# Attention: the queries' scale moves from the turning copies to the maximum pass, and the last queries move into the keys' tile

## The chip, the cores and the metric

The kernel runs on one core of one Trainium2 chip. The metric is the device time of one execution in microseconds (us); the median of several runs is compared. Engines are named as in the profile: PE (TensorE; PEld is its weight load), DVE (VectorE), ACT (ScalarE), POOL (GpSimd), SP (SyncE, which issues most transfers).

## What is computed

```python
batch, n_heads, seq, head_dim = (8, 8, 576, 64)
scale = 1.0 / np.sqrt(q.shape[-1])
scores = scale * np.matmul(q, k.transpose(0, 1, 3, 2))
thresh = np.max(scores, axis=-1, keepdims=True) - tau
scores = np.where(scores >= thresh, scores, -1000000000.0)
attn = exp(scores - max), divided by (its row sum + 1e-9)
x = (attn @ v), heads side by side: 4608 tokens x 512
h = np.maximum(x @ w_in, 0.0)          # 512 -> 2048
return (h * h @ w_out)                 # 2048 -> 512
```

All of it is computed in fp32. The two weight matrices arrive in a wide type and are converted in the kernel while the attention runs.

## The kernel before

The program has two stages, one after the other. The first is the attention, the second the two dense layers, done by a scheme that trades matrix products for sums. The change touches the attention alone.

**Units and periods.** A pair is one batch with two neighbouring heads (j = 0, 1), 32 in all. A unit is 128 queries of a pair (4 units a pair) or the last 64 queries of two pairs together; there are 144 units. A period handles two units, A and B, and also the end of earlier ones, so that there are 72 periods. What each engine gets in a period, and in which order, is written out by hand: `PLAIN` (L592) and `CONVERTING` (L597). CONVERTING is taken by the 33 periods in which weights are converted (periods 2 to 34, since two halves of a conversion lie in neighbouring periods), PLAIN by the 37 after them; periods 0 and 1 have lists of their own (`BEGIN_WITH`, L602). Every engine works through its own queue in this order; semaphores join them.

**The steps of a period.** 
- `SA` and `SB` (`scores`, L423): PE multiplies queries by keys into PSUM (`sc`, six banks). A's 576 scores per row lie in bank 0 (j = 0) and bank 5 (j = 1), with the last 64 in bank 1 or 4; B's lie in banks 2 and 3.
- `topA0` and its three fellows (`top`, L450, instruction L452): DVE reads 576 scores of a row from PSUM, writes them to SBUF (tile `s`), and accumulates the row's minimum. The scores are negated, because the scale is negative.
- `leastA` (L459, POOL) makes the threshold; `powA0` (L462, ACT) the exponentials; `maskA0` (L467, DVE) compares with the threshold, which is a value per row, multiplies, and accumulates the row's sum.
- `U`, `V`, `W` (L380, L515, PE) turn the weights 64 by 64 into PSUM, and `eU`, `eV`, `eW` (L523, ACT) copy them out.
- `PV` (L532, PE) multiplies by the values into banks 0 and 5, so it has to come behind topA0 and topA1. `x` (L659 on DVE in PLAIN, L657 on ACT in CONVERTING) copies the result out.
- `T` (`turn`, L391, instruction L398) turns the queries or the keys of a coming pair on PE, into banks 1 and 4. `eT` copies them out (L403 and L411). For queries (`which` 0) that is two ACT activations of 128x256 with the scale (L403); for keys (`which` 1) two plain ACT copies of 256 and 320 columns (L411) and one ACT activation of 64 columns (L403), the pair's last 64 queries. In the very first turn of keys DVE makes the second copy.

**Where things lie.** Turned queries are `qT` (512 columns), keys `kT` (576 columns), the last queries `qR` (64 columns). `qscale` is a column of 128 values, -1/8 for a tau that isn't negative; `read_tau` (L114) makes it at the start. The line that the maximum pass has now is

```python
made = nc.vector.tensor_scalar(
    out=s[:, j, :], in0=sc[:, ds(at, S)], scalar1=1.0, scalar2=None,
    op0=ALU.mult, op1=ALU.min, accum_out=nmx[:, j : j + 1],
)
```

Of the kernel before, what the change touches and what calls it, by code (L numbers as in the profile page):

```python
# [10 lines left out]
FP32 = mybir.dt.float32  # L11
# [3 lines left out]
AF = mybir.ActivationFunctionType  # L15
# [33 lines left out]
def kernel(  # L49
# [25 lines left out]
    nc = tc.nc  # L75
    B, H, S, D = q.shape
    P = 128
# [3 lines left out]
    FULL = S // P  # L81
    REST = S - FULL * P
    BLK = [P] * FULL + [REST]
    NB = len(BLK)
    BANK = 512
    MAIN = FULL * P
# [16 lines left out]
    sb, cv = Region(arena, 0, X_AT[0]), Region(arena, X_AT[0], ARENA)  # L103
# [7 lines left out]
    qscale = const.tile([P, 1], FP32, name="qscale")  # L111
# [160 lines left out]
    loaded, loaded_v, turned, weights = {}, {}, {}, {}  # L272
    CH = NB + FULL
    HALF = P // 2
# [57 lines left out]
    def places(i):  # L332
        if i not in turned:
            turned[i] = (
                sb.tile([P, MAIN], FP32, tag="qT", bufs=Q_RING, name="qT"),
                sb.tile([P, S], FP32, tag="kT", bufs=K_RING, name="kT"),
                sb.tile([P, REST], FP32, tag="qR", bufs=K_RING, name="qR"),
            )
        return turned[i]

# [2 lines left out]
    def ask_ahead(i, which):  # L343

        while asked[which] < min(len(pairs) - 1, i + (2 if i else 1)):
            asked[which] += 1
            (load_k if which else load_q)(asked[which])
# [4 lines left out]
    Q_RING, K_RING, W_RING = 3, 4, 2  # L352
    MEET = (("scores", "turned", (Q_RING, K_RING)), ("values", "weights", (W_RING,)), ("x", "weights", (W_RING,)))

    def touch(what, made, at, size, key=0):

        if at is None:
            return
        on = range(at // BANK, (at + size - 1) // BANK + 1)
        met = {made.ins.engine}  # L360
        for kind, other, others, its in reversed(touched):
            e = other.ins.engine
            if e == made.ins.engine:
                continue
            if on[-1] < others[0] or others[-1] < on[0]:
                if any({what, kind} == {x, y} and any((key - its) % n == 0 for n in rings) for x, y, rings in MEET):
                    continue
                tc.declare_no_dep(made.ins, other.ins, reason="other banks")
            elif e not in met:
                met.add(e)  # L370
                tc.add_manual_dep(made.ins, other.ins.name, behind, reason="same bank")
        touched.append((what, made, on, key))
        while len(touched) > 300:
            touched.popleft()
# [16 lines left out]
    def turn(i, which, spots, other=None):  # L391

        nat, to = loaded.pop((i, which)), places(i)
        of = [nat[:, t, :] for t in range(FULL)] + ([loaded.pop((i, 2))] if which else [])
        for t, x in enumerate(of):
            for r, (spot, at) in enumerate(spots):
                rows = ds(r * HALF, HALF)
                made = nc.tensor.transpose(spot[:, ts(t, HALF)], x[rows, :], ident[rows, rows])  # L398
                touch("turns", made, at, BANK)
        half = FULL * HALF  # L400

        def scaled(to, spot):
            touch("turned", nc.scalar.activation(out=to, in_=spot[0], func=AF.Identity, scale=qscale[:, :]), spot[1], BANK, i)  # L403

        def then():
            part = lambda r, x, n: (spots[r][0][:, ds(x, n)], spots[r][1])
            if which:
                for r, n in ((0, half), (1, half + REST)):
                    spot = part(r, 0, n)
                    copy_by = other if r and other else nc.scalar.copy  # L410
                    touch("turned", copy_by(to[1][:, ds(r * half, n)], spot[0]), spot[1], BANK, i)  # L411
                scaled(to[2], part(0, half, REST))
                ask_ahead(i, 1)
            else:
                for r in range(2):
                    scaled(to[0][:, ds(r * half, half)], part(r, 0, half))
                ask_ahead(i, 0)

        return then

# [2 lines left out]
    def scores(n, rest):  # L423

        of, t = units[n]
        at_k, count = (MAIN, REST) if rest else (0, MAIN)
        for j in range(2):
            first = n % 2 != j
            to = (3 * j + 1) * BANK + first * (BANK - REST) if rest else (3 * j + 2 * first) * BANK
            for c in range(2):  # L430
                rows, at = ds(j * D, D), ds(c * HALF, HALF)
                qT, kT, qR = turned[of[c]]
                lhs = qT[rows, ds((c * FULL + t) * HALF, HALF)] if t < FULL else qR[rows, :]
                made = nc.tensor.matmul(  # L434
                    sc[at, ds(to, count)], lhs, kT[rows, ds(at_k, count)], start=True, stop=True
                )
                touch("scores", made, to, count, of[c])

    def softmax(n):

        if n % 2 == 0:
            smalls[n // 2] = sb.tile([P, 4, 4], FP32, tag="small", bufs=4, name="small")
        small = smalls[n // 2]
        nmx, thr, sm = (small[:, i, ds(n % 2 * 2, 2)] for i in range(3))
        w = sb.tile([P, CH, 2, D], FP32, tag="w", bufs=4, name="w")
        s = sb.tile([P, 2, S], FP32, tag="s", bufs=2, name="s")
        weights[n] = w
        of = lambda j: s[:, j, :].rearrange("p (c d) -> p c d", d=D)

        def top(j):  # L450
            at = 3 * j * BANK + (n % 2 != j) * (2 * BANK - REST)
            made = nc.vector.tensor_scalar(  # L452
                out=s[:, j, :], in0=sc[:, ds(at, S)], scalar1=1.0, scalar2=None,
                op0=ALU.mult, op1=ALU.min, accum_out=nmx[:, j : j + 1],
            )
            touch("tops", made, at, S)

        def least():
            nc.gpsimd.tensor_scalar(out=thr, in0=nmx, scalar1=tau_p[:, :], scalar2=None, op0=ALU.add)  # L459

        def power(j):
            nc.scalar.activation(  # L462
                out=w[:, :, j, :], in_=of(j), func=AF.Exp, bias=nmx[:, j : j + 1], scale=-1.0
            )

        def mask(j):
            nc.vector.scalar_tensor_tensor(  # L467
                out=w[:, :, j, :], in0=of(j), scalar=thr[:, j : j + 1], in1=w[:, :, j, :],
                op0=ALU.is_le, op1=ALU.mult, accum_out=sm[:, j : j + 1],
            )  # L470

        def over():
            sm = small[:, 2, :]
            nc.gpsimd.tensor_scalar(out=sm, in0=sm, scalar1=1e-9, scalar2=None, op0=ALU.add)

        def inverse():
            nc.vector.reciprocal(out=small[:, 3, :], in_=small[:, 2, :])

        soft[n] = dict(top=top, least=least, power=power, mask=mask, over=over, inverse=inverse)

    def do(n, what, *args):
# [6 lines left out]
    for g in range(2, 2 * len(pairs)):  # L488
        two, x = divmod(g - 4, 4)
# [129 lines left out]
    def period(p):  # L619
# [19 lines left out]
        def turn_some():  # L639
            free = None  # L640
            if turns and p < 2:
                pq = pt_pool.tile([P, 2, BANK], FP32, tag="pt", name="pq")
                free = [(pq[:, r, :], None) for r in range(2)]
            late["turn"] = [turn(g // 2, g % 2, free or spots()) for g in turns]
# [30 lines left out]
        def scored_a():  # L675
            if has(A):
                scores(A, False)
                scores(A, True)
                scores(B_, True)
                softmax(A)  # L680
# [438 lines left out]
    with tc.manual_schedule():  # L1119
        with ExitStack() as stack:  # L1120
            sc = stack.enter_context(tc.tile_pool(name="sc", bufs=1, space=PSUM)).tile([P, 6 * BANK], FP32, name="sc")
# [114 lines left out]
        for n, (steps, h) in enumerate(PASSES):  # L1236
# [106 lines left out]
```

## Time and profile before

| | |
|---|---|
| runs (us) | 1298.04, 1300.32, 1300.54; median 1300.32 |
| profiled execution, first to last instruction (us) | 1298.2; no other time of it is listed |
| granted TensorE clock, mean | 0.997 |
| busy over the span | PE 98%, PEld 86%, DVE 78%, ACT 65%, POOL 71% |
| attention | to about 496 us; DVE busy 229.03 of 232 us in 20 to 252, 235.39 of 244 us in 252 to 496 |
| two dense layers | from about 496 us; PE busy 792.81 of 802.2 us |

A busy share tells how much of a stretch an engine had an instruction in it; it doesn't tell who waits for whom. For that, the order of one period's instructions in time is read.

### The profile page before, as it was taken

Reading aid. Unit: us, or ns where it says so; the run is one execution under the profiler, and the core shown is the slowest. Engines: PE = TensorE matmul, PEld = TensorE weight load, DVE = VectorE, ACT = ScalarE, POOL = GpSimd, SP = SyncE. Lnnn points to the kernel's source line nnn. Section 1 sums busy time; section 2 is a strip of 40 time slices with the busy share of each in tenths; the row PEclk is TensorE's granted clock in tenths of the full one; section 3 lists DMA queues with packets and bytes.
Section 4 is the critical chain, followed back from the end, with each engine's and each line's share of the span. In section 5 each row is a group of like instructions: output and inputs, shape, how many; then the busy total and the mean of one; then the engine's idle time right before and its main releaser. Section 6 shows DMA issues by size and latency. Waiting matters only on the chain.

```text
span 1298.2 us, 45819 instructions
## 1 busy us (share of the span) xinstructions
PE 1276.4 (98%) x18287; PEld 1117.7 (86%) x18287; DVE 1007.0 (78%) x2423; ACT 845.5 (65%) x1498; POOL 926.8 (71%) x1031
## 2 busy tenths in 40 slices
PE   8999999999999999999999999999999999999998
PEld 5777777677777778988888888999999999999998
DVE  6999999999999996886887878867646654665463
ACT  6999999888998984666765856675523432343240
POOL 2787878755555321888897989858787767777775
PEclk8999999999999999999999999999999999999999
DMA  5665566544333312667768768589554224522411
GB/s 143 163 160 154 153 192 180 149 103 110 85 79 80 92 34 64 191 183 218 212 186 226 218 175 235 162 304 391 195 159 164 83 86 159 163 80 88 160 34 34
DMA packets 291413, 196.20 MB, mean 151 GB/s; under 512 B 100096, under 2 KB 252160, under 8 KB 291200
## 3 DMA queue, kind: packets, MB, share of 16 engines
q1 hardware_dynamic: 289888, 192.87, 51.5%
q8 instruction: 144, 2.36, 0.8%
q14 instruction: 69, 0.57, 0.2%
q10 hardware_dynamic: 1312, 0.41, 0.1%
HBM read 120.85 MB, written 72.35 MB: 149 GB/s over the span
## 4 chain that ended last, share of the span: by engine, by line
PE 86%; ACT 5%; DVE 4%; DMA 3%; issue 2%; POOL 0%; SPq 0%; ACTq 0%; DVEq 0%; POOLq 0%
PE po L1077 28%; PE ph L935 16%; PE sc L532 11%; PE sc L434 10%; PE ph L942 10%; PE pt L380 6%; DVE arena L452 2%; PE sc L515 2%; PE sc L398 2%; ACT arena L462 1%; ACT arena L523 1%; DMA g<-arena 1%; PE sc L380 1%; DVE arena L125 1%; DMA wall<-w 1%
## 5 line engine op out<-in xcount | busy, mean ns | idle before, releaser
L125 POOL TENSOR_TENSOR arena<-arena 128x512 f32<-128x512 f32 (+1 forms) x314 | 378.1, 1222 | 147.0 <-DVE arena L125 119.3
L1077 PE MATMUL po<-wall,arena 128*128 128x128 f32 x3528 | 395.0, 275 | 1.9 <-ACT arena L752 1.4
L1077 PEld LDWEIGHTS po<-wall,arena 128*128 128x128 f32 x3528 | 394.4, 192 | 2.5 <-ACT arena L752 1.8
L125 DVE TENSOR_TENSOR arena<-ph,arena 128x512 f32<-128x512 f32 x378 | 255.1, 689 | 79.9 <-PE ph L935 31.5
L122 POOL TENSOR_TENSOR arena<-arena 128x128 f32<-128x128 f32 (+1 forms) x322 | 265.4, 825 | 23.0 <-DMA arena<-w 6.6
L935 PE MATMUL ph<-arena,wall 128*128 128x256 f32 x1176 | 256.6, 380 | 1.8 <-DVE arena L125 1.4
L935 PEld LDWEIGHTS ph<-arena,wall 128*128 128x128 f32 x1176 | 222.2, 190 | 35.9 <-DVE arena L125 5.4
L125 DVE TENSOR_TENSOR arena<-po,arena 128x128 f32<-128x128 f32 x378 | 108.2, 290 | 167.7 <-PE po L1077 163.4
L467 DVE SCALAR_TENSOR_TENSOR arena<-arena 128x576 f32<-128x576 f32 x288 | 235.7, 855 | 0.9 <-ACT arena L462 0.9
L791 ACT COPY c<-arena 128x512 f32<-128x512 f32 (+1 forms) x295 | 169.0, 578 | 71.8 <-DVE arena L122 35.8
L452 DVE TENSOR_SCALAR_CACHE_REDUCE arena<-sc 128x576 f32<-128x576 f32 x288 | 205.1, 748 | 10.9 <-ACT arena L523 4.3
L462 ACT ACTIVATE arena<-arena 128x576 f32<-128x576 f32 x288 | 208.7, 773 | 7.4 <-DVE arena L452 4.2
L532 PEld LDWEIGHTS sc<-arena 64*64 64x64 f32 x5760 | 159.2, 133 | 36.5 <-DVE arena L452 19.8
L532 PE MATMUL sc<-arena 64*64 64x128 f32 (+1 forms) x5760 | 180.5, 262 | 2.9 <-DVE arena L452 1.3
L434 PE MATMUL sc<-arena 64*64 64x64 f32 (+1 forms) x2304 | 176.2, 415 | 3.8 <-ACT arena L403 2.4
L523 ACT COPY arena<-pt 128x1024 f32<-128x1024 f32 x144 | 146.4, 1016 | 27.9 <-PE pt L380 26.5
L122 DVE TENSOR_TENSOR arena<-arena,c 128x512 f32<-128x512 f32 x235 | 154.4, 666 | 11.0 <-ACT c L791 7.6
L752 ACT COPY arena<-po 128x128 f32<-128x128 f32 x63 | 16.6, 264 | 186.4 <-PE po L1077 183.7
L942 PE MATMUL ph<-arena,wall 128*128 128x128 f32 x1176 | 132.0, 275 | 0.7 <-DVE arena L659 0.7
L942 PEld LDWEIGHTS ph<-arena,wall 128*128 128x128 f32 x1176 | 131.6, 192 | 1.1 <-issue 0.8
L380 PEld LDWEIGHTS pt<-ident,arena 64*128 64x128 f32 x2304 | 83.5, 139 | 40.0 <-ACT arena L523 30.1
L434 PEld LDWEIGHTS sc<-arena 64*64 64x64 f32 x2304 | 74.0, 134 | 42.2 <-issue 14.1
(54 smaller groups left out, 1079.7 us busy)
## 6 DMA issues: line engine op xcount, KB each, us to landing
arena<-g SPq DMA_DIRECT2D x144, 256.0 KB, 4.4
g<-arena SPq DMA_DIRECT2D x192, 128.0 KB, 2.9
w<-arena SPq DMA_DIRECT2D x60, 256.0 KB, 2.8
wall<-w SPq DMA_DIRECT2D x49, 256.0 KB, 5.2
g<-arena SPq DMA_DIRECT2D x48, 256.0 KB, 3.8
arena<-w SPq DMA_DIRECT2D x44, 256.0 KB, 3.3
arena<-in_v_dram SPq DMA_DIRECT2D x32, 288.0 KB, 3.8
out_dram<-arena SPq DMA_DIRECT2D x70, 128.0 KB, 2.2
```

What stands on the lines that cost most here:

```text
L122: e.tensor_tensor(out=out, in0=x, in1=y, op=ALU.subtract)
L125: e.tensor_tensor(out=out, in0=x, in1=y, op=ALU.add)
L380: made = nc.tensor.transpose(pt[:, r, ts(slot, HALF)], of[rows, :], ident[rows, rows])
L434: made = nc.tensor.matmul(sc[at, ds(to, count)], lhs, kT[rows, ds(at_k, count)], start=True, stop=True)
L452: made = nc.vector.tensor_scalar(out=s[:, j, :], in0=sc[:, ds(at, S)], scalar1=1.0, scalar2=None, op0=ALU.mult, op1=ALU.min, accum_out=nmx ...
L462: nc.scalar.activation(out=w[:, :, j, :], in_=of(j), func=AF.Exp, bias=nmx[:, j : j + 1], scale=-1.0)
L467: nc.vector.scalar_tensor_tensor(out=w[:, :, j, :], in0=of(j), scalar=thr[:, j : j + 1], in1=w[:, :, j, :], op0=ALU.is_le, op1=ALU.mult, a ...
L532: made = nc.tensor.matmul(sc[ds(u * D, D), ds(5 * j * BANK + row, count)], loaded_v[i][rows, (c - (u != j)) % CH, :], wT[m][rows, ds(weigh ...
L791: nc.scalar.copy(c, y)
L935: nc.tensor.matmul(to[:, 2 * j : 2 * j + 2, :], W_IN[m, k][:, ts(2 * h + j, P)], part_x(steps, k, m), start=(not more and j == 0), stop=Tr ...
L942: nc.tensor.matmul(to[:, j, :], W_IN[m, k][:, ts(j, P)], x, start=(not more and j == 0), stop=True, skip_group_check=True,)
L1077: nc.tensor.matmul(to, g[:, j, :], w[:, j, :], start=(not more and j == 0), stop=(j == 3), skip_group_check=True)
```

## The change

The maximum pass multiplies by `qscale`, a column in SBUF, where it multiplied by the constant 1.0. The turned queries are no longer scaled: `eT` is two plain ACT copies for queries (256 columns each) and two for keys (320 columns each). The keys' tile gets 640 columns in two halves of 320: the first half ends with the pair's last 64 queries, the second with the last 64 keys. So the keys that a main score product reads are two pieces of 256 columns with a gap of 64. `qR` is gone; the SBUF taken is the same. PE, POOL and SP have the same instructions in the same order; DVE has the same instructions, the 288 of L452 with another operand; ACT has 32 fewer.

```diff
-                sb.tile([P, MAIN], FP32, tag="qT", bufs=Q_RING, name="qT"),
-                sb.tile([P, S], FP32, tag="kT", bufs=K_RING, name="kT"),
-                sb.tile([P, REST], FP32, tag="qR", bufs=K_RING, name="qR"),
+                sb.tile([P, 2, MAIN // 2], FP32, tag="qT", bufs=Q_RING, name="qT"),
+                sb.tile([P, 2, MAIN // 2 + HALF], FP32, tag="kT", bufs=K_RING, name="kT"),
...
-            if which:
-                for r, n in ((0, half), (1, half + REST)):
-                    spot = part(r, 0, n)
-                    copy_by = other if r and other else nc.scalar.copy
-                    touch("turned", copy_by(to[1][:, ds(r * half, n)], spot[0]), spot[1], BANK, i)
-                scaled(to[2], part(0, half, REST))
-                ask_ahead(i, 1)
-            else:
-                for r in range(2):
-                    scaled(to[0][:, ds(r * half, half)], part(r, 0, half))
-                ask_ahead(i, 0)
+            for r, (spot, at) in enumerate(spots):
+                copy_by = other if r and other else nc.scalar.copy
+                touch("turned", copy_by(to[which][:, r, :], spot[:, 0 : len(of) * HALF]), at, BANK, i)
+            ask_ahead(i, which)
...
-                lhs = qT[rows, ds((c * FULL + t) * HALF, HALF)] if t < FULL else qR[rows, :]
+                lhs = qT[rows, c, ts(t, HALF)] if t < FULL else kT[rows, 0, MAIN // 2 :]
+                into, rhs = sc[at, ds(to, count)], kT[rows, 1, MAIN // 2 :]
+                if not rest:
+                    into, rhs = into.rearrange("p (r n) -> p r n", r=2), kT[rows, :, 0 : MAIN // 2]
...
-                out=s[:, j, :], in0=sc[:, ds(at, S)], scalar1=1.0, scalar2=None,
+                out=s[:, j, :], in0=sc[:, ds(at, S)], scalar1=qscale[:, :], scalar2=None,
```

More of the change, by code (lines that the diff above doesn't have):

```diff
@@ L399, in turn @@
                 touch("turns", made, at, BANK)
-        half = FULL * HALF
-        def scaled(to, spot):
-            touch("turned", nc.scalar.activation(out=to, in_=spot[0], func=AF.Identity, scale=qscale[:, :]), spot[1], BANK, i)
         def then():
-            part = lambda r, x, n: (spots[r][0][:, ds(x, n)], spots[r][1])
-            if which:
-                for r, n in ((0, half), (1, half + REST)):
-                    spot = part(r, 0, n)
-                    copy_by = other if r and other else nc.scalar.copy
-                    touch("turned", copy_by(to[1][:, ds(r * half, n)], spot[0]), spot[1], BANK, i)
-                scaled(to[2], part(0, half, REST))
-                ask_ahead(i, 1)
-            else:
-                for r in range(2):
-                    scaled(to[0][:, ds(r * half, half)], part(r, 0, half))
-                ask_ahead(i, 0)
+            for r, (spot, at) in enumerate(spots):
+                copy_by = other if r and other else nc.scalar.copy
+                touch("turned", copy_by(to[which][:, r, :], spot[:, 0 : len(of) * HALF]), at, BANK, i)
+            ask_ahead(i, which)
         return then
@@ L425, in scores @@
         of, t = units[n]
-        at_k, count = (MAIN, REST) if rest else (0, MAIN)
+        count = REST if rest else MAIN
         for j in range(2):
@@ L431, in scores @@
                 rows, at = ds(j * D, D), ds(c * HALF, HALF)
-                qT, kT, qR = turned[of[c]]
-                lhs = qT[rows, ds((c * FULL + t) * HALF, HALF)] if t < FULL else qR[rows, :]
-                made = nc.tensor.matmul(
-                    sc[at, ds(to, count)], lhs, kT[rows, ds(at_k, count)], start=True, stop=True
-                )
+                qT, kT = turned[of[c]]
+                lhs = qT[rows, c, ts(t, HALF)] if t < FULL else kT[rows, 0, MAIN // 2 :]
+                into, rhs = sc[at, ds(to, count)], kT[rows, 1, MAIN // 2 :]
+                if not rest:
+                    into, rhs = into.rearrange("p (r n) -> p r n", r=2), kT[rows, :, 0 : MAIN // 2]
+                made = nc.tensor.matmul(into, lhs, rhs, start=True, stop=True)
                 touch("scores", made, to, count, of[c])
```

## Prediction, on record before the result

> **What bounds the kernel now.** I read four views in this order: busy times by stretch, to see which engine has no room; the instructions of one period in time, to see who waits; the groups by shape, for prices; the waits. The dense layers (from 496 us) are untouched and start when the attention ends, so what the attention loses or gains is the kernel's. The busy times of the two halves of the attention (columns: stretch, its length, then PE, PEld, DVE, ACT, POOL with the number of instructions, PE clock, DMA share, GB/s):
>
> ```profile
> 20.00:252.00 232.00, 227.95 (x5579) 170.20 (x5572) 229.03 (x615) 221.55 (x395) 182.01 (x223) 0.99 0.61 161
> 252.00:496.00 244.00, 240.78 (x6346) 181.15 (x6348) 235.39 (x707) 218.25 (x341) 119.83 (x172) 1.00 0.36 84
> ```
>
> In the converting half DVE has 229.03 of 232 us, in the plain half 235.39 of 244. One converting period on DVE, from its first top to the next period's first (start, duration, line, operation):
>
> ```profile
> 128.99 0.75 DVE L452 TENSOR_SCALAR_CACHE_REDUCE arena<-sc 128x576 f32<-128x576 f32 x1
> ...
> 129.67 0.75 DVE L452 TENSOR_SCALAR_CACHE_REDUCE arena<-sc 128x576 f32<-128x576 f32 x1
> ...
> 131.70 0.42 DVE L227 TENSOR_SCALAR arena<-arena 128x512 int32<-128x512 int32 x1
> 132.04 0.17 DVE L477 RECIPROCAL arena<-arena 128x4 f32<-128x4 f32 x1
> 132.13 0.78 DVE L467 SCALAR_TENSOR_TENSOR arena<-arena 128x576 f32<-128x576 f32 x1
> ...
> 136.06 0.75 DVE L452 TENSOR_SCALAR_CACHE_REDUCE arena<-sc 128x576 f32<-128x576 f32 x1
> ```
>
> No row here carries an idle note: from 128.99 to 136.06 each instruction starts as the one before lets go. **A converting period is 7.07 us of DVE and nothing else**; what is added to a DVE instruction is added to the period. A plain period differs:
>
> ```profile
> 310.08 0.76 DVE L452 TENSOR_SCALAR_CACHE_REDUCE arena<-sc 128x576 f32<-128x576 f32 x1 [0.28 <-ACT arena L523]
> ...
> 310.76 0.75 DVE L452 TENSOR_SCALAR_CACHE_REDUCE arena<-sc 128x576 f32<-128x576 f32 x1
> ...
> 311.59 0.76 DVE L452 TENSOR_SCALAR_CACHE_REDUCE arena<-sc 128x576 f32<-128x576 f32 x1
> ...
> 312.27 0.18 DVE L477 RECIPROCAL arena<-arena 128x4 f32<-128x4 f32 x1
> 312.36 0.73 DVE L452 TENSOR_SCALAR_CACHE_REDUCE arena<-sc 128x576 f32<-128x576 f32 x1
> ```
>
> topA0 starts at 310.08 (the named releaser, L523, had ended by 309.74; what ended last is PE's turn T, about 0.1 us before). topA1 follows after 0.68, topB0 only after 0.83: it waits 0.15 us for PE's SB. On PE, PV's first product (bank 0) starts at 311.30, its product for bank 5 at 311.58, 0.06 after topA1 ends at 311.52: PE stalls some 0.2 us for topA1. The loop of a plain period is T, topA0, topA1, PV, the rest of PE, T. Its plain periods last 6.35 to 7.16 us, 6.57 on average.
>
> **The price of a column in place of a constant.** No DVE instruction before differs in only that. The nearest rows (columns: shape, count, busy us, mean ns; the first two from 260 to 490 us, the others from the whole span):
>
> ```profile
> L467 DVE SCALAR_TENSOR_TENSOR arena<-arena 128x576 f32<-128x576 f32 x140 | 109.0, 815 | 0.0
> L452 DVE TENSOR_SCALAR_CACHE_REDUCE arena<-sc 128x576 f32<-128x576 f32 x141 | 102.8, 748 | 7.8 <-ACT arena L523 4.3
> ```
>
> ```profile
> L235 DVE SCALAR_TENSOR_TENSOR arena<-arena 128x512 int32<-128x512 int32 x32 | 21.8, 682 | 0.0
> L122 DVE TENSOR_TENSOR arena<-arena,c 128x256 f32<-128x256 f32 x12 | 4.9, 411 | 0.0
> ```
>
> The mask (L467) has a column as scalar, the top (L452) a constant; both have 576 elements and an accumulator. The mask takes 815 - 748 = 67 ns more, and 0.74 against 0.68 us from start to start in the timeline, which is what the queue feels: 62 ns in the medians (739 and 677). Is that its second input? L235 is the mask's kind of instruction with a constant and two inputs; at 1.05 ns an element (L122: 512 elements 680, 256 elements 411) it would take 682 + 64 x 1.05 = 749 ns for 576, as long as the top. So a second input costs nothing, and the mask's broken pattern (9 pieces of 64) hardly does: L122 takes the same time whole and in pieces of 128. What is left is the column. **I take 62 ns.** From below: 0, if the column is read while the instruction before still runs. From above: ACT's rows, where L403 (128x256 with a column) takes 458 ns and L411 (a copy of the same size) 355: 103 ns, though these differ in kind too.
>
> The Trainium skill ("ScalarE: Activation LUTs", section "What ACT_TABLE_LOAD costs") says that each pointer operand of one value per partition adds about 93 ns to an ACTIVATE; the 103 ns here agree roughly. By that price, carried over to DVE as an estimate, the sum below would be 20 us and not 13. It speaks of ACT alone.
>
> **The change part by part.**
> - *Tops, converting*: 33 periods x 4 tops x 62 ns = 8.2 us, all exposed, since DVE has no idle time there. Periods 0 and 1 likewise: 2 x 0.248 = 0.5 us.
> - *Tops, plain*: topA0 and topA1 stand in the loop and make PV 2 x 62 = 0.124 us later. The 0.15 us ahead of topB0 hides the same 0.124 from DVE's own queue; topB0 and topB1 then add 0.124 to DVE, whose masks end just ahead of the next T, so both queues grow alike. 37 x 0.124 = 4.6 us. If PE took up half of it elsewhere, 2.3; if DVE bore all four, 9.2.
> - *ACT*: a pair's queries save 2 x (458 - 355) = 0.21 us, its keys 355 + 426 + 325 - 2 x 426 = 0.25 us: 32 x 0.46 = 14.7 us of ACT. In the converting half DVE's full queue hides all of it. In the plain half ACT has 218.25 of 244 us and waits 18.7 us for PE; eT lies behind powers whose masks are already served, and the turned tiles are needed a period or more later. I cost the gain at 0; if the cover went, the rival below has its size.
> - *Start*: the first score product waits for L411 then L403 (7.41 to 8.00); one copy of 426 ns ends at 7.84, but DVE's 0.49 copy of the second half ends at 7.93. Gain 0.1 us.
> - *Keys in two pieces*: PE's L935 reads pieces of 128 columns and takes 380 ns for 256 columns, L942 275 for 128: a cost by column, none by piece seen. 0. The 30 waits on ACT that the last score products get are for copies that the same period's main products already waited for, or older ones: 0.
> - *SP, POOL*: same order; the loads are asked for behind eT as before. 0.
>
> Sum: 8.2 + 0.5 + 4.6 - 0.1 = 13.2 us. On the profiled execution 1298.2 + 13.2 = 1311.4. Its span lies 2.1 us under the median of the runs, and the forecast is for a median: 1300.3 + 13.2 = **1313.5**.
>
> **The rivals.**
> - *The column is free* (read beside the instruction before). Then nothing changes but the start: 1300.2. For it: ACT and DVE instructions overlap their neighbours by some 80 ns, which might cover it. Against: the mask has the same overlap and still takes 62 ns more.
> - *The column costs what it does on ACT*, 103 ns: 33 x 0.412 + 2 x 0.412 + 37 x 0.206 = 22.0: 1322.3. Against: no DVE row shows such a step.
> - *The column meets POOL.* Today tops read PSUM only. A mask, which reads SBUF, takes 1.20 us in place of 0.81 once in every converting period, each time beginning as POOL's L212 (2.03 us) runs. topB1 (131.02) starts inside POOL's L219 (130.62 to 131.23). If it then waited for L219's end, 0.21 x 33 = 6.9 us come on top: 1320.4. It decides only if POOL's L219 shuts DVE out as L212 seems to.
> - *The other side: ACT was the plain half's hidden limit and the column is free.* PE's products waited for L403 and L523 there:
>
> ```profile
> PEld sc L434 <- ACT arena L403: 11.8, 30, 0.6
> ...
> PE sc L434 <- ACT arena L403: 1.7, 4, 0.4
> ...
> PE pt L380 <- ACT arena L523: 1.0, 4, 0.3
> ```
>
>  If shorter copies take these away, 1.7 + 1.0 = 2.7 us go: 1297.6; with the weight loads' 11.8 too, 1285.8. It decides if the price of the column is under 2.7 / 206 = 13 ns (206 exposed tops: 4 x 33 + 2 x 37). Against: those weight loads wait while the product before them (512 columns) still streams, so PE isn't idle.
>
> **How the numbers follow.** About 0.2% (2.6 us) can be told from no change. Forecast, 62 ns give or take 20 with one to two plain tops exposed in each pair (1307 to 1319): 0.62. Free column: 0.18. ACT's price: 0.06. POOL: 0.05. Other side: 0.09. So slower 0.73, same 0.18, faster 0.09. The range runs from 1299 (it holds most of the free case) to 1320 (it holds the forecast's upper end and half of POOL's case); what is left out, ACT's price, the other side and some edges, is about 0.2.
>
> **What would show it.** The tops' mean of 748 ns should be about 810, and their distance in a converting period 0.74 us in place of 0.68; a converting period 7.32 us, a plain one about 6.70; PE's wait for topA1 ahead of PV some 0.3 us; ACT's busy time 14 us less without any other engine starting sooner; the dense layers as long as before. It is wrong if the tops keep their 748 ns, if they show two lengths (POOL), or if plain periods shorten although the tops grew.

## The result and the profile after

The changed kernel takes 1309.99 us (median of 4 runs, 1307.53 to 1311.34), the kernel before in the same comparison 1299.18 us (median of 4 runs, 1297.27 to 1300.54): 10.8 us more, a ratio of 1.0083 with a 95% interval of 1.0066 to 1.0100. Forecast were 13.2 us, 1313.5. The sign and the main term held; the sum was some 2 us too large. The profiled execution is the quickest of the four: its span is 1305.7 us, its own time 1307.53. So the two traces lie only 7.5 us apart (1298.2 and 1305.7), and where a total counts it is taken from the runs.

The line numbers are those of the changed kernel: tops L440 (were L452), masks L455 (L467), scores L424 (L434), `PV` L520 (L532), the turned tiles' copies L403, the other evictions L511 (L523). First the busy times by stretch, cut where the converting half and the attention now end (columns as before):

```profile
20.00:260.00 240.00, 231.10 (x5643) 171.68 (x5638) 238.19 (x621) 222.00 (x385) 182.38 (x226) 1.00 0.60 157
260.00:505.00 245.00, 242.41 (x6262) 178.18 (x6259) 240.58 (x698) 212.46 (x320) 118.62 (x169) 1.00 0.35 82
505.00:1305.70 800.70, 792.73 (x6234) 757.09 (x6226) 531.77 (x1074) 395.22 (x745) 621.35 (x627) 1.00 0.55 169
```

PE's busy time in the last stretch is what it was (792.73 us, before 792.81). The attention, from the start of its first score product to the start of its last product (`PV`), went from 498.74 to 508.84 us; the loss lies there. That last product starts at 506.82 us before and at 516.36 after, about 11 us behind the cuts at 496 and 505, which mark the end of the score products. From its end to the end of the span, the dense layers take 791.2 us before and 789.2 after. In the traces of the experiments this is 789.1 to 792.5. The four kernels with the joined tile have the four shortest (789.1 to 789.5, the others 790.0 to 792.5); whether the tile has to do with it isn't settled, and the runs' totals don't show it (e2_copies and e7_old_tiles below). DVE is still full in the first half (238.19 of 240) and fuller than before in the second (240.58 of 245, before 235.39 of 244).

One converting period on DVE (start, duration, engine, line, operation, shapes):

```profile
138.93 0.81 DVE L440 TENSOR_SCALAR_CACHE_REDUCE arena<-sc,qscale 128x576 f32<-128x576 f32 x1
...
139.67 0.81 DVE L440 TENSOR_SCALAR_CACHE_REDUCE arena<-sc,qscale 128x576 f32<-128x576 f32 x1
...
141.89 0.42 DVE L227 TENSOR_SCALAR arena<-arena 128x512 int32<-128x512 int32 x1
...
143.03 1.24 DVE L455 SCALAR_TENSOR_TENSOR arena<-arena 128x576 f32<-128x576 f32 x1
...
146.28 0.81 DVE L440 TENSOR_SCALAR_CACHE_REDUCE arena<-sc,qscale 128x576 f32<-128x576 f32 x1
```

`qscale` now stands among the top's inputs, its duration is 0.81 us where it was 0.75, and the next top starts 0.74 us later where it started 0.68 later. From top to top the period is 146.28 - 138.93 = 7.35 us; before it was 7.07. Of the 0.28 us the four tops have 0.25, from start to start; the slow mask (143.03), which was there before with 1.20 us, has the rest. The median of the converting periods is 7.32.

Periods 0 and 1 are another matter. The last mask of period 1 and the first top of period 2, first in the kernel before, then in the changed one:

```profile
20.59 0.82 DVE L467 SCALAR_TENSOR_TENSOR arena<-arena 128x576 f32<-128x576 f32 x1 [0.31 <-ACT arena L462]
...
22.86 0.76 DVE L452 TENSOR_SCALAR_CACHE_REDUCE arena<-sc 128x576 f32<-128x576 f32 x1 [1.44 <-PE sc L398]
```

```profile
20.14 0.82 DVE L455 SCALAR_TENSOR_TENSOR arena<-arena 128x576 f32<-128x576 f32 x1
...
22.32 0.82 DVE L440 TENSOR_SCALAR_CACHE_REDUCE arena<-sc,qscale 128x576 f32<-128x576 f32 x1 [1.35 <-PE sc L397]
```

DVE stands idle here, by 0.31 and 1.44 us in the kernel before, and the longer tops use up part of that: from the first top of period 0 to that of period 2 it is 13.33 us before, 13.36 after, and 13.33 in e1_ones, which has the column alone. The prediction counted these eight tops as exposed.

In a plain period DVE and PE read so (all engines, the lines in question):

```profile
323.49 0.82 DVE L440 TENSOR_SCALAR_CACHE_REDUCE arena<-sc,qscale 128x576 f32<-128x576 f32 x1
...
324.23 0.81 DVE L440 TENSOR_SCALAR_CACHE_REDUCE arena<-sc,qscale 128x576 f32<-128x576 f32 x1
...
324.71 2.58 PE L520 MATMUL sc<-arena 64*64 64x128 f32 x72
...
325.01 0.82 DVE L440 TENSOR_SCALAR_CACHE_REDUCE arena<-sc,qscale 128x576 f32<-128x576 f32 x1
...
325.10 1.95 PEld L520 LDWEIGHTS sc<-arena 64*64 64x64 f32 x70 [0.25 <-DVE arena L440]
```

PV's first product (bank 0) starts at 324.71, but topA1 ends only at 324.23 + 0.81 = 325.04, and the loads for bank 5 wait for it. From PV's first product to topA1's end it is 0.33 us; in the period shown of before it was 311.52 - 311.30 = 0.22. topB0 now starts 0.78 after topA1, 0.04 of it idle, where it was 0.83 with 0.15 idle. So the column's time ahead of PV is on the path, and topB0's gap takes up part of it on DVE.

The groups by shape from 260 to 495 us, and the waits from 262 to 490 us (engine, line waited with, releaser: total us, times, longest):

```profile
L455 DVE SCALAR_TENSOR_TENSOR arena<-arena 128x576 f32<-128x576 f32 x142 | 110.3, 814 | 0.0
L440 DVE TENSOR_SCALAR_CACHE_REDUCE arena<-sc,qscale 128x576 f32<-128x576 f32 x140 | 109.1, 809 | 3.8 <-issue 2.7
```

```profile
PEld sc L520 <- DVE arena L440: 22.1, 68, 1.1
...
PEld sc L424 <- ACT arena L403: 7.5, 28, 0.3
...
PE sc L520 <- DVE arena L440: 0.5, 2, 0.3
```

The top now takes as long as the mask (809 and 814 ns). The waits of `PV`'s weight loads for tops doubled (before 11.2 us, 37 times, in the same window). And one line of before is gone, the one that the prediction showed as its rival's: PE's own wait for L403, 1.7 us in 4 places. This is one of the four places in the kernel before, and then the same place in the changed one:

```profile
347.83 1.32 PE L434 MATMUL sc<-arena 64*64 64x512 f32 x24 [0.41 <-ACT arena L403]
```

```profile
354.42 0.62 ACT L403 COPY arena<-sc 128x256 f32<-128x256 f32 x2
...
355.09 1.32 PE L424 MATMUL sc<-arena 64*64 64x512 f32 x24
```

The score products for the next unit stood 0.41 us behind the scaled copies of their queries (two activations, 0.81 us together, from 346.97). The two plain copies take 0.62 us, and PE's products start without a wait of their own.

### The profile page after: what moved, and what is told of

Its sections match the earlier page's. It is cut to its first block, busy times and chain, and to the rows that moved or that the text cites. A ratio compares the mean times of both kernels' runs of the same rounds, so it can differ in the third digit from the quotient of the medians.

```text
span 1305.7 us, 45801 instructions
## 1 busy us (share of the span) xinstructions
PE 1280.8 (98%) x18287; PEld 1116.0 (85%) x18287; DVE 1022.3 (78%) x2423; ACT 840.6 (64%) x1466; POOL 925.4 (71%) x1031
## 4 chain that ended last, share of the span: by engine, by line
PE 88%; DVE 5%; ACT 3%; issue 2%; DMA 1%; SPq 0%; POOL 0%; DVEq 0%; POOLq 0%; ACTq 0%
PE po L1065 29%; PE ph L923 17%; PE sc L520 12%; PE sc L424 10%; PE ph L930 10%; PE pt L379 5%; DVE arena L440 4%; PE sc L503 2%; PE sc L397 2%; ACT arena L450 1%; PE sc L379 1%; DMA g<-arena 1%; ACT c L779 1%; ACT arena L892 0%; ACT arena L511 0%
## 5 line engine op out<-in xcount | busy, mean ns | idle before, releaser
L455 DVE SCALAR_TENSOR_TENSOR arena<-arena 128x576 f32<-128x576 f32 x288 | 235.5, 854 | 0.2 <-ACT arena L450 0.2
L440 DVE TENSOR_SCALAR_CACHE_REDUCE arena<-sc,qscale 128x576 f32<-128x576 f32 x288 | 221.1, 808 | 7.0 <-issue 2.7
L450 ACT ACTIVATE arena<-arena 128x576 f32<-128x576 f32 x288 | 212.1, 774 | 12.7 <-DVE arena L440 8.4
L520 PEld LDWEIGHTS sc<-arena 64*64 64x64 f32 x5760 | 159.4, 133 | 49.0 <-DVE arena L440 38.9
L520 PE MATMUL sc<-arena 64*64 64x128 f32 (+1 forms) x5760 | 186.2, 262 | 9.2 <-DVE arena L440 7.6
L424 PE MATMUL sc<-arena 64*64 64x64 f32 (+1 forms) x2304 | 176.5, 414 | 2.0 <-DVE arena L403 0.7
L511 ACT COPY arena<-pt 128x1024 f32<-128x1024 f32 x144 | 146.6, 1018 | 34.4 <-PE pt L379 32.7
L424 PEld LDWEIGHTS sc<-arena 64*64 64x64 f32 x2304 | 73.6, 134 | 41.0 <-issue 20.6
```

Of the source, the lines that this page charges most:

```text
L424: made = nc.tensor.matmul(into, lhs, rhs, start=True, stop=True)
L440: made = nc.vector.tensor_scalar(out=s[:, j, :], in0=sc[:, ds(at, S)], scalar1=qscale[:, :], scalar2=None, op0=ALU.mult, op1=ALU.min, accu ...
L450: nc.scalar.activation(out=w[:, :, j, :], in_=of(j), func=AF.Exp, bias=nmx[:, j : j + 1], scale=-1.0)
L455: nc.vector.scalar_tensor_tensor(out=w[:, :, j, :], in0=of(j), scalar=thr[:, j : j + 1], in1=w[:, :, j, :], op0=ALU.is_le, op1=ALU.mult, a ...
L520: made = nc.tensor.matmul(sc[ds(u * D, D), ds(5 * j * BANK + row, count)], loaded_v[i][rows, (c - (u != j)) % CH, :], wT[m][rows, ds(weigh ...
```

## The experiments

To see where each microsecond sits, the period is read from topA0 to the next topA0. The table has the median of the 33 converting ones and means of 36 plain ones (the last of the 37 has no top behind it) by kind: the four in which eT copies queries that the next products wait for (they end at topA0 of periods 40, 49, 58 and 67, "long"), the four after them, without a turn, the four after those, and the other 24. "Plain, all" is from topA0 of period 35 to that of period 71. The converting half is compared by its median, because in most traces, that of before too, one to three periods, nearly all between topA0 of period 27 and that of period 33, are by themselves up to 1.8 us longer, at places that differ from trace to trace.

| us | before | after | e1_ones | e2_copies | e3_mask_const | e4_plain_a | e5_plain_b | e6_conv_a | e7_old_tiles |
|---|---|---|---|---|---|---|---|---|---|
| converting | 7.07 | 7.32 | 7.35 | 7.07 | 6.89 | 7.07 | 7.07 | 7.20 | 7.07 |
| plain, long | 7.15 | 6.96 | 7.15 | 6.90 | 7.18 | 7.09 | 7.28 | 7.15 | 6.90 |
| plain, no turn | 6.35 | 6.47 | 6.47 | 6.35 | 6.17 | 6.47 | 6.41 | 6.35 | 6.35 |
| plain, after those | 6.45 | 6.48 | 6.51 | 6.41 | 6.39 | 6.47 | 6.56 | 6.45 | 6.42 |
| plain, other 24 | 6.53 | 6.67 | 6.65 | 6.53 | 6.53 | 6.66 | 6.55 | 6.54 | 6.53 |
| plain, all | 236.5 | 239.8 | 240.2 | 235.3 | 235.6 | 240.0 | 238.2 | 236.6 | 235.3 |
| ratio to before | | 1.0083 | 1.0088 | 0.9986 | 0.9953 | 1.0022 | 1.0017 | 1.0022 | 0.9988 |
| its interval | | 1.0066 to 1.0100 | 1.0071 to 1.0105 | 0.9975 to 0.9996 | 0.9937 to 0.9969 | 1.0012 to 1.0032 | 1.0007 to 1.0028 | 1.0012 to 1.0033 | 0.9979 to 0.9998 |

The theory was: the column's 61 ns make the whole loss, in the converting half through DVE's full queue, in the plain half through topA0 and topA1 ahead of PV; the shorter copies give back a little where PE waits for them. Its rivals: the price isn't the column's, or not all of it; plain periods go by DVE's whole queue, so that unit B's tops count as A's do; and what was given back comes from the joined tile, not from the missing scale.

### The column alone, with ones (e1_ones)

The kernel before, with a column of ones in the tops.

```diff
+    ones_c = const.tile([P, 1], FP32, name="ones_c")
+    nc.gpsimd.memset(ones_c[:, :], 1.0)
...
-                out=s[:, j, :], in0=sc[:, ds(at, S)], scalar1=1.0, scalar2=None,
+                out=s[:, j, :], in0=sc[:, ds(at, S)], scalar1=ones_c[:, :], scalar2=None,
```

> The kernel before, with its scaled copies and its tiles as they were; only the tops multiply by a column of ones in SBUF in place of the constant 1.0. Theory (the column costs some 61 ns on DVE, and nothing else in the change costs time): tops 808 ns on average, an undisturbed converting period 7.32 us where it was 7.07, most plain periods 0.12 us longer, and the five long plain periods (7.15) longer too, since the copies are as before: 33 x 0.245 + 36 x 0.124 = 12.5 us, a ratio near 1.0096, so a little more than the whole change cost. Rival (the new layout of the keys, or the plain copies, cost part of the loss): clearly less than the change's 10.8 us, say 7.

Measured: 1310.67 us, ratio 1.0088. On the page of this kernel the tops are:

```profile
L454 DVE TENSOR_SCALAR_CACHE_REDUCE arena<-sc,ones_c 128x576 f32<-128x576 f32 x288 | 221.2, 807 | 6.9 <-ACT arena L525 2.4 <-PE sc L436 1.6 <-PE sc L400 1.1
```

807 ns, where the constant 1.0 had 748. The column alone makes the whole loss, converting and plain. Its long periods stay at 7.15 us, though: there the path doesn't go through topA0 and topA1 alone, and PE's wait for L403 is still in them.

### The copies alone (e2_copies)

The changed kernel, with a constant in the tops.

```diff
-                out=s[:, j, :], in0=sc[:, ds(at, S)], scalar1=qscale[:, :], scalar2=None,
+                out=s[:, j, :], in0=sc[:, ds(at, S)], scalar1=-SCALE, scalar2=None,
```

> The changed kernel with the constant -1/8 in the tops where it had the column, so the copies and the tiles of the change alone (the case of a negative tau, for which the column is 0, is left out). Theory: tops back at 748 ns; converting periods 7.07 us; the four or five plain periods of 7.15 us fall to about 6.85, because score products no longer wait for the scaled copies, 1.2 to 1.6 us in all; with the start 1.3 to 2 us under the kernel before, ratio 0.9985 to 0.999. Rival (keys in two pieces or the extra waits cost PE time): at or above the kernel before. Rival (ACT was a hidden limit all along the plain half): 3 us or more under it.

Measured: 1296.85 us, ratio 0.9986, the fastest here apart from e3_mask_const, which leaves part of the work out, and faster than both kernels. Converting periods are those of before (7.07). In the plain half the long ones are shorter, 7.15 to 6.90, and those after them a little, 6.45 to 6.41; the same place as above in this kernel:

```profile
346.19 1.32 PE L424 MATMUL sc<-arena 64*64 64x512 f32 x24 [0.16 <-ACT arena L403]
```

The wait fell from 0.41 to 0.16 us, 0.25 us less, and the period is 0.25 us shorter: 1.0 us in the four of them, of 1.2 us in the plain half. So ACT's gain isn't nothing, as the forecast had it, but nearly all of it comes from where PE stands idle for a copy. ACT's busy time fell by 10.6 us (845.5 to 834.9), and most of that bought nothing.

### A constant in the masks (e3_mask_const)

If the 62 ns belong to the column, taking it from the masks must give them back.

```diff
-                out=w[:, :, j, :], in0=of(j), scalar=thr[:, j : j + 1], in1=w[:, :, j, :],
+                out=w[:, :, j, :], in0=of(j), scalar=1e30, in1=w[:, :, j, :],
```

> The kernel before, where the masks compare with the constant 1e30 in place of the threshold's column (so nothing is masked and the thresholds are made but not read; the masks also lose their wait for POOL). It tests the price from the other end. Theory (the 62 ns between mask and top are the column): masks about 750 ns where they were 811 to 815, start to start 0.68 where it was 0.74; a converting period 4 x 0.062 = 0.25 us shorter, 6.82; plain periods nearly as before, because the masks aren't in the loop from T over topA0 and topA1 to PV: 8 us less in all, ratio 0.994. Rival (the mask's 62 ns are its second input or its broken pattern): masks and time as before. Rival (plain periods go by the sum of DVE's work): 36 x up to 0.25 more, some 15 us less in all.

Measured: 1292.23 us, ratio 0.9953, 6.2 us less. The masks fell from 855 to 794 ns in the mean. Four lines of one converting period on DVE:

```profile
128.22 0.73 DVE L467 SCALAR_TENSOR_TENSOR arena<-arena 128x576 f32<-128x576 f32 x1
...
128.88 1.19 DVE L467 SCALAR_TENSOR_TENSOR arena<-arena 128x576 f32<-128x576 f32 x1
...
130.01 0.75 DVE L467 SCALAR_TENSOR_TENSOR arena<-arena 128x576 f32<-128x576 f32 x1
...
131.29 0.74 DVE L467 SCALAR_TENSOR_TENSOR arena<-arena 128x576 f32<-128x576 f32 x1
```

A mask with a constant takes 0.74 us, as a top with a constant does, and 0.68 us from start to start: the column's price holds for another kind of instruction. Neither the second input nor the broken pattern costs anything that shows, unless it is made up by the mask's reading SBUF where the top reads PSUM, which no run here takes apart. The period is 0.18 us shorter and not 4 x 0.062 = 0.25: the second mask (128.88) still takes 1.19 us, so three masks gave something. In the plain periods DVE was given 0.25 us, too, and the 24 stayed what they were (6.53); those without a turn are 0.18 us shorter and those after them 0.06, the long ones 0.03 longer. **DVE's sum isn't what a plain period goes by**, although its busy share there is 96%.

### The column in half of the plain tops (e4_plain_a, e5_plain_b)

e1_ones with the column in topA0 and topA1 of the plain periods alone; then in topB0 and topB1 alone (`n % 2 == 1`).

```diff
-                out=s[:, j, :], in0=sc[:, ds(at, S)], scalar1=1.0, scalar2=None,
+                out=s[:, j, :], in0=sc[:, ds(at, S)], scalar1=ones_c[:, :] if n >= 4 and n % 2 == 0 and not converts(n // 2) else 1.0, scalar2=None,
```

> The kernel before, with a column of ones only in the tops of unit A (topA0, topA1) and only in the plain periods. Theory (PV waits for topA1, so these two stand in the loop): most plain periods 0.12 us longer, 36 x 0.124 = 4.5 us, ratio 1.0034; the stall of PE ahead of PV grows from some 0.17 to 0.29 us; converting periods as before. Rival (plain periods go by the sum of DVE's work and the 0.15 us ahead of topB0 takes up what topA0 and topA1 add): no change in the plain periods.

> The kernel before, with a column of ones only in the tops of unit B (topB0, topB1) and only in the plain periods; the counterpart of the run with unit A. Theory (only what makes topA1 end later lengthens a plain period): no turn-bearing plain period longer by more than 0.03 us, since its masks end 0.1 to 0.2 us ahead of the next topA0; only the seven periods without a turn, in which DVE is the later one, grow by 0.12 us: under 1 us in all, ratio 1.0005. Rival (the plain half goes by the sum of DVE's work): as much as unit A's run, 0.12 us a period, 4 us, ratio 1.003.

Measured: 1301.56 us (1.0022) and 1301.70 us (1.0017). The totals don't tell them apart, the periods do. Unit A's columns make the plain half 3.5 us longer, as much as all four columns do (e1_ones: 3.6), and the kinds "no turn" and "other" grow by 0.12 and 0.13, as with all four. Unit B's columns leave the other 24 nearly alone (6.55, of which 0.02 is one period that is 0.44 us longer by itself), as expected. The long ones, though, grow by 0.12, and the kind after the next by 0.11, where at most 0.03 was expected; the periods without a turn grow by 0.06 and not 0.12. The chain that fits in the long ones is another: topB1, its powers on ACT, eT behind them in ACT's queue, and then the score products that wait for eT. PE's wait for L403 in the four places fits it: 1.7 us before, 2.2 with unit B's columns. The plain half grows by 1.7 us, where under 1 was expected; this trace also has two converting periods of 8.77 and 8.27 us, in which no top has a column.

So unit A's tops count and B's mostly don't, as the forecast's loop has it; it is wrong for the long periods. Columns of A and B don't simply add there (7.09 with A alone, 7.28 with B alone, 7.15 with both). With A's column PE's wait for L403 falls from 1.7 to 1.0 us, 0.18 a period, so more than the 0.12 that `PV` comes later; with both it is 1.2 us, 0.12 less a period, and the two even out. Why it falls by more than 0.12 with A alone isn't settled.

### The column in half of the converting tops (e6_conv_a)

The same line with the condition `n % 2 == 0 and converts(n // 2)`.

> The kernel before, with a column of ones only in the tops of unit A and only in the converting periods. Theory (there a period is the sum of DVE's instructions): half of the full step, 2 x 0.061: undisturbed converting periods 7.19 us where they were 7.07, 33 x 0.122 = 4.0 us, ratio 1.003, plain periods as before. Rival (there too it is the way from topA1 to PV): the full step of 0.245, 7.32 us and 8 us.

Measured: 1302.34 us, ratio 1.0022. One period on DVE:

```profile
138.28 0.81 DVE L454 TENSOR_SCALAR_CACHE_REDUCE arena<-sc,ones_c 128x576 f32<-128x576 f32 x1
...
139.02 0.81 DVE L454 TENSOR_SCALAR_CACHE_REDUCE arena<-sc,ones_c 128x576 f32<-128x576 f32 x1
...
139.76 0.75 DVE L454 TENSOR_SCALAR_CACHE_REDUCE arena<-sc 128x576 f32<-128x576 f32 x1
...
140.43 0.75 DVE L454 TENSOR_SCALAR_CACHE_REDUCE arena<-sc 128x576 f32<-128x576 f32 x1
...
145.47 0.81 DVE L454 TENSOR_SCALAR_CACHE_REDUCE arena<-sc,ones_c 128x576 f32<-128x576 f32 x1
```

139.02 - 138.28 = 0.74 and 139.76 - 139.02 = 0.74 with the column, 140.43 - 139.76 = 0.67 without, in neighbouring instructions of one kernel. The period is 7.19 us, halfway between 7.07 and 7.35: in the converting half it is the sum of DVE, whichever top has the column.

### Plain copies in the old tiles (e7_old_tiles)

The kernel before, with plain copies for the queries and the last queries, and a constant in the tops. The tiles stay apart.

```diff
-            touch("turned", nc.scalar.activation(out=to, in_=spot[0], func=AF.Identity, scale=qscale[:, :]), spot[1], BANK, i)
+            touch("turned", nc.scalar.copy(to, spot[0]), spot[1], BANK, i)
...
-                out=s[:, j, :], in0=sc[:, ds(at, S)], scalar1=1.0, scalar2=None,
+                out=s[:, j, :], in0=sc[:, ds(at, S)], scalar1=-SCALE, scalar2=None,
```

> The kernel before with its old tiles (the last queries in a tile of their own, three copies for keys), where only the scale moved: the copies of queries are plain copies, the tops multiply by the constant -1/8 (the case of a negative tau is left out). Theory (the copies' gain is that the plain copies of queries end sooner, in the four plain periods that had 7.15 us): these four at 6.90 us as in the run of the copies alone, the total 1 to 2 us under the kernel before, ratio 0.9985 to 0.9992. Rival (the gain comes from the joined tiles, with one ACT instruction fewer for keys): the four at 7.15 us, the total as before.

Measured: 1297.43 us, ratio 0.9988, within e2_copies' interval, with the same periods. The gain is the missing scale in the copies; the joined tile, the keys in two pieces and the extra waits neither cost nor give anything that these runs can tell.

### Two other orders for the converting half (e8_low_words_early, e9_both_early)

In nearly every converting period (32 of 33 before) one mask takes 1.2 us in place of 0.8. If POOL's L212 (the conversion's step `c2`) holds it, moving `c2` should free 0.4 us a period, 13 us in all. Both start from e2_copies.

```diff
-        fetch SA U eU T SB topA0 s1 c1 topA1 topB0 c3 V PV leastA over powA0 topB1
-        powA1 powB0 c4 eT inv x maskA1 maskA0 W leastB maskB0 c5 eV c2 powB1 c6 eW maskB1 xm
+        fetch SA U eU T SB topA0 s1 c1 topA1 topB0 V PV leastA over c2 powA0 topB1
+        powA1 powB0 c4 eT inv x maskA1 maskA0 W leastB c3 maskB0 c5 eV powB1 c6 eW maskB1 xm
```

> The run of the copies alone (constant -1/8, plain copies, new tiles; negative tau left out), with the order of the converting periods changed: POOL's product of the low words (L212 of the kernel before) comes behind the threshold of unit A, while DVE runs tops, and the clamp (L219) behind the threshold of unit B. In every converting period one mask took 1.13 us where the others took 0.74, starting 0.88 us after that product. Theory (the converting period is the sum of DVE's instructions, and POOL's product holds back a mask that starts in its first 0.9 us, but no top): all masks near 0.74; the converting period 0.2 to 0.39 us shorter, 6.7 to 6.85 us; 7 to 13 us less, ratio 0.990 to 0.995 against the kernel before. Rival (POOL's product holds back tops too): one top takes 1.1 us in place of the mask and the period stays at 7.07. Rival (the thresholds come late behind the product): DVE idle ahead of masks for POOL, period as before or longer.

Measured: 1306.07 us, ratio 1.0050 (1.0036 to 1.0064), so longer, and the converting period 7.36 us (median). The mask that was to be freed starts 0.49 us into L212 in the trace of e2_copies, not 0.88 as said above. In the new order L212 no longer holds a mask, but another mask is held instead (all engines, the lines in question):

```profile
149.33 0.87 POOL L447 TENSOR_SCALAR arena<-arena,tau_p 128x2 f32<-128x2 f32 x1
...
150.17 0.61 POOL L219 TENSOR_SCALAR arena<-arena 128x512 f32<-128x512 f32 x1
150.23 1.15 DVE L455 SCALAR_TENSOR_TENSOR arena<-arena 128x576 f32<-128x576 f32 x1
```

The mask that starts 0.06 us behind POOL's L219 takes 1.15 us, and the threshold ahead of it (L447) takes 0.87 us beside a mask, where the trace of before has 0.38 and 0.29. MaskB0, which needs this threshold, starts 0.18 us later than it would right behind the mask before it, as the second rival had it. L227, which now starts 0.41 us into L212, takes 0.58 us where it took 0.42. With 0.18 and 0.16 more and a held mask that is 0.05 shorter than before, the period is 0.29 us longer. e9_both_early moves both conversion steps ahead of the masks, and `xm`, POOL's product, behind `leastB`. Its list in full:

```diff
+        fetch SA U eU T SB topA0 s1 c1 topA1 c3 leastA over c2 topB0 V PV powA0 topB1
+        powA1 powB0 c4 eT inv x maskA1 maskA0 W leastB xm maskB0 c5 eV powB1 c6 eW maskB1
```

> Again the run of the copies alone (constant -1/8, plain copies, new tiles; negative tau left out) with another order for POOL in the converting periods: the clamp (L219), the threshold of unit A and the product of the low words (L212) all right behind topA1, then the threshold of unit B and the attention's output product, then the last step of the conversion. Theory, as the run before left it (POOL's one-input instructions over 512 columns hold back a DVE instruction that starts early in them and reads SBUF, a mask or L227, and no top; a converting period is the sum of DVE's instructions): no mask of 1.13 or 1.15 us any more, L227 some 0.16 us longer, so the period 0.15 to 0.3 us shorter than 7.07; 5 to 10 us less, ratio 0.992 to 0.996 against the kernel before. Rival (unit B's threshold, behind the product, comes later than its mask could start): what the mask gains is lost as idle time ahead of maskB0, the period stays within 0.05 us of 7.07.

Measured: 1307.83 us, ratio 1.0072 (1.0056 to 1.0087), longer again, the converting period 7.38 us (median), and again with a held mask, now behind `xm` (L657):

```profile
154.19 0.87 POOL L447 TENSOR_SCALAR arena<-arena,tau_p 128x2 f32<-128x2 f32 x1
...
155.02 0.73 POOL L657 TENSOR_TENSOR arena<-arena 128x256 f32<-128x256 f32 x1
155.09 1.28 DVE L455 SCALAR_TENSOR_TENSOR arena<-arena 128x576 f32<-128x576 f32 x1
```

Here, too, the late threshold costs 0.18 us ahead of maskB0, as the rival said, but the period didn't stay at 7.07. Both misses say the same: which POOL instruction comes last ahead of a mask changes, the held mask doesn't go. How the two engines hold each other back in full stays open, and neither of the two orders avoids it.

## Why the prediction was right, and where it was off

- *The column's price, 62 ns.* Right: the mean went from 748 to 808 ns, the distance of neighbouring tops from 678 to 739 ns in the median, 61. It was taken from a row of another kind of instruction (the mask), after L235 had shown that the second input costs nothing; e3_mask_const bore out this reading of the mask. All tops of the changed kernel lie between 780 and 820 ns.
- *Converting, 8.2 us, all exposed.* Right: 33 x 0.25 = 8.2 by the medians, and half of it with half of the columns (e6_conv_a). Summed over the trace it is only 241.1 - 234.4 = 6.7. Two converting periods in the trace of before took 8.10 and 7.37 us, one in that of after 7.67, and period 2 fell from 7.16 to 6.65; in the other traces it is 6.59 to 7.28, whatever their tops.
- *Periods 0 and 1, 0.5 us.* Not there: 13.33 us before and 13.36 after. That DVE has no idle time was read from a later period; here it waits for PE and ACT.
- *Plain, 4.6 us through topA0 and topA1.* Right for most periods, 0.12 us each against the forecast 0.124, and it is A's tops (e4_plain_a). The 36 periods measured 239.8 - 236.5 = 3.3, and the start of the attention's last product lies 0.1 us further behind the last topA0: 3.4.
- *ACT's gain, costed at 0.* **This is the main step that failed.** It said that the turned tiles are needed a period or more later. In the four long plain periods PE's score products wait for the queries that eT has just copied. The forecast has 7.15 + 0.12 = 7.27 us for such a period; measured are 6.96. Of the 0.31, 0.12 is the column's own, which costs nothing there while PE waits for L403 (e1_ones: 7.15 with the column as without), and 0.19 is the copies' (7.15 to 6.96; with the constant 7.15 to 6.90). Four times 0.31 is 1.2 us, as much as the plain half fell short by. That the rest evens out is in part luck: the four periods "after those" grew by 0.03 us in place of 0.12, and two single periods among the other 24 by 0.31 and 0.33. The rival "ACT was the plain half's hidden limit" had named this wait, 1.7 us in 4 places; it was real, but stood beside the column's price and not in its stead.
- *topB0 and topB1 hidden in plain periods.* Right for most, wrong in the long ones and the two kinds after them (e5_plain_b). That both queues grow alike isn't the reason: DVE has room there, since with unit B's columns alone the 24 stay at 6.55 us.
- *Start, -0.1 us.* Can't be told: the first score product started at 8.08 us before and 7.51 after, but between 7.40 and 8.47 in the other traces, whatever their copies.
- *Keys in two pieces, the extra waits, SP and POOL, 0 each.* Nothing in the runs speaks against it (e7_old_tiles beside e2_copies).
- *The rivals.* The free column and ACT's 103 ns are out by the tops' 808 ns; POOL's case too, since the tops have one length, whatever POOL does. In the converting half of the changed kernel 61 tops start inside L245, 31 inside L657 and 20 inside L219 (most of these in its last 0.03 us), and all take 801 to 818 ns.
- *ACT's busy time, 14 us less.* It fell by 4.9 (845.5 to 840.6). Against the kernel with the column alone it is 852.8 - 840.6 = 12.2: the column makes the powers wait for tops oftener (8.4 us beside 4.2). That instructions which don't follow each other directly overlap less would fit; it wasn't measured.

In sum 8.2 + 3.4 = 11.6 by the periods, 10.8 (8.6 to 13.0) by the runs. The forecast's 13.2 lies just above the upper end; the 0.5 of periods 0 and 1 and the 1.2 of the long plain periods are what it had too much, as far as the periods show.

## What to carry to other kernels

Price a new operand on the engine that each stage goes by: here 288 x 61 ns = 17.6 us more on DVE cost about 11 us (e1_ones), and 10.6 us less on ACT gave back about 2 (e2_copies). A scale that is known when the kernel is built belongs in a constant: in the maximum pass it was free (747 ns). Before a saving on a second engine is put at nothing, look through the waits for the few places where the bounding engine itself, and not its weight load, waits for that engine: here 4 of 36 periods held 1.0 of the 1.2 us. And idle time has to be looked for in every stretch that a price is counted in, the short one at the start too.

## What the runs showed of the hardware

- A column of one value per partition as DVE's scalar costs 61 ns over a constant in an instruction of 128x576 (no other size was tried), the same for a source in PSUM (tops, 748 to 808 ns) and in SBUF (masks, 0.81 to 0.74 us). It isn't hidden by the instruction before, although neighbours overlap by about 70 ns (0.81 long, 0.74 apart), and POOL doesn't hold it up (801 to 818 ns beside L245, L657 and L219).
- On ACT the step is larger: a scaled activation of 128x256 takes 455 to 458 ns, a plain copy of the same size from the same place 358 to 362, some 96 ns less, though the two differ in kind too (ACTIVATE and COPY). The 93 ns that the Trainium skill gives for such an operand ("ScalarE: Activation LUTs", section "What ACT_TABLE_LOAD costs") agree with this.
- A mask that starts shortly after a POOL instruction is held: 0.39 us behind L212 (it starts 0.48 us into it), 0.34 behind L219, 0.47 behind L657. A top, which reads PSUM, never was, with or without the column. The Trainium skill ("SBUF — State Buffer", section "SBUF: two separate sides") says that DVE instructions with two SBUF inputs and POOL's that read SBUF take turns on a port pair, and that the one that starts first keeps it for the whole instruction. That masks are held, which have two SBUF inputs, and tops aren't agrees. The whole instruction doesn't agree by the trace's times: behind L219 (0.61 us, 0.06 of it past) 0.55 were to be waited and 0.34 were, though spans on POOL are rough.
- Masks aren't alone in it. L235, which has two SBUF inputs as well, took 1.15 and 1.23 us in place of 0.68 in the two places of e3_mask_const where it starts 0.45 us into L212. L227, with one SBUF input, takes 0.58 us in place of 0.42 where it starts 0.41 us into L212 (e8_low_words_early); what holds it isn't settled.
- It works the other way round as well: POOL's threshold (L447) takes 0.87 us where it starts beside a running mask (e8_low_words_early, e9_both_early) in place of 0.29 and 0.38. L212 takes 2.03 us where a mask starts 0.49 us into it (e2_copies) and 1.63 where the first mask beside it mostly starts 1.0 us into it (e9_both_early).
